# Attention results put in row order by 0/1 matmuls and stored as one transfer of 512-byte rows

## The chip, the cores and the metric

The kernel runs on one core of a Trainium2 chip. The metric is the device time of one execution in microseconds (us). Times are given as the median of several runs. A percentage is the mean time of one kernel's fast runs over that of the other kernel's fast runs of the same rounds, with a 95% interval, so it is not quite the ratio of the medians quoted beside it. In the experiments that mean leaves out each kernel's first, profiled run, which the medians include.

## The reference

Grouped-query attention with 16 batches, 32 query heads on 8 K/V heads, 16 query rows, 2048 keys, D = 128, all bf16:

```python
k = jnp.repeat(k, rep, axis=1); v = jnp.repeat(v, rep, axis=1)   # rep = 4
scores = jnp.einsum("bhqd,bhkd->bhqk", q, k) * D ** -0.5
p = softmax(scores, axis=-1)
return jnp.einsum("bhqk,bhkd->bhqd", p, v)
```

K and V are 67 MB each and are read once; the result is 2.1 MB. One K/V head with its 4 x 16 = 64 query rows is a *group*; there are 128 groups.

## The kernel before

Two groups make a *pair* (64 pairs), two pairs a *step* (32 steps, 4 groups). A static list schedule, computed when the kernel is built, gives each engine a fixed order of operations. SyncE (SP) issues all loads and nearly all stores, in one fixed order; K and V share 15 slots of 1 MB, and a load is issued when its slot comes free.

```python
NSLOT = 15; NBO = 9      # load slots; result buffers O
LAG = 6; DSTORE = 12     # V(p) is loaded 6 pairs after K(p); a store is queued 12 pairs after its V
QCH = 1024; QLEAD = 5    # Q comes in 8 chunks, loaded 5 pairs ahead
# ... the order of SP's transfers:
for t in range(NP + LAG):
    if t < NP:
        dma.append(("K", t))
    if qstep.get(t, 0):
        dma.append(("Q", qstep[t]))
    if t >= LAG:
        dma += v_of(t - LAG)
    if t - LAG - DSTORE in range(0, NP, 2):
        dma.append(("ST", (t - LAG - DSTORE) // 2))
```

For each pair: DVE transposes K in 32x32 blocks, PE makes the scores S, ACT takes the exponential (P), PE transposes P, DVE or ACT evicts that to PT, PE multiplies with V (PV, in `O_ps`), and ACT or DVE scales by 1/rowsum into O. Partition 64·gg + m of an O buffer holds row m of group 4·step + 2·gg + pair, and the two pairs of a step lie side by side in the free dimension:

```python
Osb = [sb(f"O{i}", [128, 2, 128], BF16) for i in range(NBO)]
# ... the normal store of a step (transfers, SP): two transfers, 64 partitions x 2 rows of 256 B each
for gg in range(2):
    g = 4 * x + 2 * gg
    sp.dma_start(of[64 * g:64 * (g + 2), :].rearrange("(p m) d -> m p d", p=2),
                 Osb[x % NBO][64 * gg:64 * (gg + 1), :, :]).then_inc(*prog_sem(prog, op))
# ... at the end, each engine: redo everything in a safe form if a row sum was out of range
eng.br_eq(reg, all_within, on_true=after, on_false=redo).branch_hint(hints[me])
```

Partition m holds row m of two *different* groups, so neither of its two rows has its neighbour in memory beside it: the store is made of 256-byte pieces.

## Time and profile before

| | before |
|---|---|
| time, median | 348.36 us (348.19 to 348.55, 3 runs) |
| span of the profiled execution | 346.9 us |
| DMA | 139.2 MB, 401 GB/s over the span |
| PE, DVE, ACT busy | 69%, 65%, 65% |

The page of the kernel before: the lines of the DMA slices (40 slices of the span; the digit is the busy share in tenths), the packets, the queues (packets, MB, share of 16 engines), and the chain that ended last.

```profile
PE 238.6 (69%) x5378; PEld 172.7 (50%) x5378; DVE 225.8 (65%) x377; ACT 226.6 (65%) x369; POOL 29.0 (8%) x35
...
DMA  7999999999999999999999999999999999999983
GB/s 309 426 412 415 411 413 412 412 415 414 411 418 415 412 412 414 415 413 414 413 412 417 414 415 414 414 413 415 413 413 414 412 417 416 414 412 412 392 336 108
DMA packets 37349, 139.21 MB, mean 401 GB/s; under 512 B 11440, under 2 KB 11440, under 8 KB 29104
...
q1 hardware_dynamic: 37216, 138.41, 98.9%
q8 instruction: 43, 0.70, 0.8%
...
DMA 72%; DVE 11%; PE 9%; ACT 6%; issue 1%; SPq 0%; ACTq 0%
```

DMA is at 9 from the second slice to the 38th, and the chain spends 72% of the span on it, nearly all on loads of K. No compute engine is above 70%. `q8 instruction` is the fetching of instructions in 43 pieces of 16 KB, on the same DMA engines as the loads. The list of issues on the same page (issue, count, size, median time from issue to landing):

```profile
slot<-in_k_dram SPq DMA_DIRECT2D x64, 1024.0 KB, 17.6
...
out_dram<-O SPq DMA_DIRECT2D x62, 32.0 KB, 13.2
```

A megabyte takes 2.5 us to move and lands 17.6 us after its issue: about seven loads are queued at any time. SP's waits for slots therefore cost nothing as long as that queue doesn't run dry.

Busy time by stretch before (windows view: window, length, busy us of each engine with instruction counts, granted clock, DMA share, GB/s):

```profile
110.00:300.00 190.00, 131.95 (x3008) 95.29 (x3008) 121.57 (x204) 127.09 (x210) 15.98 (x16) 0.94 1.03 414
...
324.00:347.00 23.00, 16.75 (x418) 12.96 (x414) 10.30 (x29) 10.57 (x18) 0.00 (x0) 0.95 0.72 260
```

The last K lands at 323.5 us; the last 23 us are a tail in which the last eight pairs get their PV and their result.

### The profile page before, as it was taken

Reading aid. Unit: us, or ns where it says so; the run is one execution under the profiler, and the core shown is the slowest. Engines: PE = TensorE matmul, PEld = TensorE weight load, DVE = VectorE, ACT = ScalarE, POOL = GpSimd, SP = SyncE. Lnnn points to the kernel's source line nnn. Section 1 sums busy time; section 2 is a strip of 40 time slices with the busy share of each in tenths; the row PEclk is TensorE's granted clock in tenths of the full one; section 3 lists DMA queues with packets and bytes.
Section 4 is the critical chain, followed back from the end, with each engine's and each line's share of the span. In section 5 each row is a group of like instructions: output and inputs, shape, how many; then the busy total and the mean of one; then the engine's idle time right before and its main releaser. Section 6 shows DMA issues by size and latency. Waiting matters only on the chain.

```text
span 346.9 us, 11937 instructions
## 1 busy us (share of the span) xinstructions
PE 238.6 (69%) x5378; PEld 172.7 (50%) x5378; DVE 225.8 (65%) x377; ACT 226.6 (65%) x369; POOL 29.0 (8%) x35
## 2 busy tenths in 40 slices
PE   1568868756686668766687665865857757576785
PEld 1345646534464446543465453643645545454564
DVE  4867996874775666746666655767559476576544
ACT  4496887665586575946759646787558746477551
POOL 1310031000400004000040000400004000000000
PEclk9998999999899898999989989999899989899899
DMA  7999999999999999999999999999999999999983
GB/s 309 426 412 415 411 413 412 412 415 414 411 418 415 412 412 414 415 413 414 413 412 417 414 415 414 414 413 415 413 413 414 412 417 416 414 412 412 392 336 108
DMA packets 37349, 139.21 MB, mean 401 GB/s; under 512 B 11440, under 2 KB 11440, under 8 KB 29104
## 3 DMA queue, kind: packets, MB, share of 16 engines
q1 hardware_dynamic: 37216, 138.41, 98.9%
q8 instruction: 43, 0.70, 0.8%
q14 instruction: 10, 0.08, 0.1%
q10 hardware_dynamic: 80, 0.02, 0.0%
HBM read 136.31 MB, written 2.10 MB: 399 GB/s over the span
## 4 chain that ended last, share of the span: by engine, by line
DMA 72%; DVE 11%; PE 9%; ACT 6%; issue 1%; SPq 0%; ACTq 0%
DMA slot<-in_k_dram 72%; DVE KT L354 9%; PE O_ps L468 3%; ACT P L373 2%; PE PT_ps L462 2%; PE S_ps L452 2%; PE QT_ps L440 1%; ACT QT L399 1%; DVE PT L399 1%; ACT PT L399 1%; DMA Qn<-in_q_dram 1%; DVE O L390 1%; ACT L360 0%; ACT Qr L360 0%; DVE rowsum L379 0%
## 5 line engine op out<-in xcount | busy, mean ns | idle before, releaser
L354 DVE STREAM_TRANSPOSE KT<-slot 128x1024 int32<-128x1024 int32 x128 | 154.5, 1231 | 101.3 <-DMA slot<-in_k_dram 92.8
L373 ACT ACTIVATE P<-S_ps 128x1024 bf16<-128x1024 f32 x128 | 130.5, 1025 | 87.5 <-PE PT_ps L462 49.6
L462 PE MATMUL PT_ps<-ident,P 128*128 128x128 bf16 x1024 | 74.4, 229 | 83.1 <-DVE PT L399 44.0
L462 PEld LDWEIGHTS PT_ps<-ident,P 128*128 128x128 bf16 x1024 | 62.3, 102 | 104.7 <-DVE PT L399 53.7
L452 PE MATMUL S_ps<-KT,QT 32*64 32x512 bf16 x2048 | 75.9, 401 | 11.0 <-ACT P L373 9.7
L468 PE MATMUL O_ps<-slot,PT 128*64 128x128 bf16 x2048 | 76.7, 233 | 1.3 <-DVE O L390 1.0
L468 PEld LDWEIGHTS O_ps<-slot,PT 128*64 128x64 bf16 x2048 | 65.9, 119 | 17.8 <-issue 14.2
L399 ACT ACTIVATE PT<-PT_ps 128x1024 bf16<-128x1024 bf16 x60 | 61.1, 1019 | 3.0 <-PE PT_ps L462 2.1
L360 POOL COPY Qr<-Qn 128x1024 bf16<-128x1024 bf16 x28 | 28.0, 1042 | 235.2 <-DMA Qn<-in_q_dram 235.2
L399 DVE COPY PT<-PT_ps 128x1024 bf16<-128x1024 bf16 x68 | 45.2, 668 | 1.8 <-PE PT_ps L462 1.8
L452 PEld LDWEIGHTS S_ps<-KT,QT 32*64 32x64 bf16 x2048 | 28.1, 106 | 32.3 <-ACT P L373 12.9
L440 PE MATMUL QT_ps<-ident,Qr 128*128 128x128 bf16 x256 | 22.1, 236 | 10.2 <-ACT Qr L360 6.1
L399 ACT ACTIVATE QT<-QT_ps 128x1024 bf16<-128x1024 bf16 x23 | 23.5, 1023 | 7.3 <-PE QT_ps L440 7.3
L373 ACT ACTIVATION_READ_ACCUMULATOR P<-S_ps 128x1 f32 x128 | 25.9, 202 | 0.0
L440 PEld LDWEIGHTS QT_ps<-ident,Qr 128*128 128x128 bf16 x256 | 16.7, 105 | 16.5 <-issue 8.3
L388 ACT ACTIVATE O<-O_ps,rrec 128x128 bf16<-128x128 f32 x27 | 9.9, 367 | 11.6 <-PE O_ps L468 11.6
L390 DVE TENSOR_SCALAR O<-O_ps,rrec 128x128 bf16<-128x128 f32 x37 | 12.0, 324 | 5.5 <-PE O_ps L468 5.4
L399 DVE COPY QT<-QT_ps 128x1024 bf16<-128x1024 bf16 x9 | 10.9, 1209 | 1.8 <-PE QT_ps L440 1.8
L379 DVE TENSOR_TENSOR rowsum<-rhalf 128x1 f32<-128x1 f32 x64 | 8.5, 152 | 4.4 <-ACT P L373 4.4
L384 DVE RECIPROCAL rrec<-rowsum 128x1 f32<-128x1 f32 x64 | 8.5, 153 | 0.5
L360 ACT ACT_TABLE_LOAD x1 | 1.3, 1283 | 3.6 <-DMA Qn<-in_q_dram 3.6
L360 DVE COPY Qr<-Qn 128x1024 bf16<-128x1024 bf16 x2 | 1.3, 690 | 3.5 <-DMA Qn<-in_q_dram 3.5
(13 smaller groups left out, 4.2 us busy)
## 6 DMA issues: line engine op xcount, KB each, us to landing
slot<-in_k_dram SPq DMA_DIRECT2D x64, 1024.0 KB, 17.6
slot<-in_v_dram SPq DMA_DIRECT2D x63, 1024.0 KB, 17.7
Qn<-in_q_dram SPq DMA_DIRECT2D x8, 256.0 KB, 15.3
out_dram<-O SPq DMA_DIRECT2D x62, 32.0 KB, 13.2
slot<-in_v_dram SPq DMA_DIRECT2D x2, 512.0 KB, 12.3
out_dram<-O SPq DMA_DIRECT2D x3, 16.0 KB, 1.8
out_dram<-O ACTq DMA_DIRECT2D x1, 16.0 KB, 2.0
```

Of the source, the lines that this page charges most:

```text
L354: ins = eng.transpose(KT[p % NKT][:, gg, :, h], prog.slot(("K", 2 * p + gg))[:, J * 64 * h:J * 64 * (h + 1)])
L360: ins = eng.activation(dst, src, ACT.Copy) if me == "act" else eng.tensor_copy(dst, src)
L373: ins = eng.activation(P[p % 2][:, :].rearrange("m (r a h j) -> m h a r j", h=2, a=2, j=32)[:, h], src.rearrange("m (a r j) -> m a r j", a ...
L379: ins = eng.tensor_tensor(rowsum[:, p:p + 1], rhalf[:, p, 0:1], rhalf[:, p, 1:2], op=ALU.add)
L384: ins = eng.reciprocal(rrec[:, p:p + 1], rowsum[:, p:p + 1])
L388: ins = eng.activation(dst, src, ACT.Copy, scale=r)
L390: ins = eng.tensor_scalar(dst, src, r, None, op0=ALU.mult)
L399: ins = eng.activation(dst, src, ACT.Copy) if me == "act" else eng.tensor_copy(dst, src)
L440: ins = pe.transpose(QT_ps[:, 128 * i:128 * (i + 1)], Qr[:, x, i, :], ident[:, :],)
L452: ins = pe.matmul(S_ps[64 * gg:64 * (gg + 1), 512 * a:512 * (a + 1)], QT[c % 2][32 * a:32 * (a + 1), x, row:row + 64], kt[:, :, x // 2, p ...
L462: ins = pe.transpose(PT_ps[h][:, 128 * t:128 * (t + 1)], P[p % 2][:, 128 * r:128 * (r + 1)], ident[:, :])
L468: ins = pe.matmul(O_ps[64 * gg:64 * (gg + 1), 0:128], PT[p % NPT][:, r, 64 * gg:64 * (gg + 1)], prog.v_rows(p)[:, gg, r, :], start=(r == 0 ...
```

## The change

The intent: make the store cheaper for the DMA engines. For each step, 8 small matmuls with columns of the identity (weights 0 and 1) copy O into PSUM so that each partition holds two neighbouring rows; an eviction writes them to `Orow`; one transfer of 128 partitions x 512 B, contiguous in memory, stores the step. The matmuls borrow the PSUM bank `QT_ps` of the Q transposes, so Q chunks must fit between two steps, and Q is loaded 10 pairs ahead instead of 5. Cut to its core:

```diff
+NOS = 3
-NBO = 9
+NBO = 7
-DSTORE = 12
+DSTORE = 10
-QLEAD = 5
+QLEAD = 10
...
+            add(("op", s), ("nm", p - 1), ("nm", p), opt(s >= 1, ("oe", s - 1)), ("qe", chunk, 3))
+            add(("oe", s), ("op", s), opt(s >= NBO, ("ST", s - NBO)))
+            add(("ST", s), ("oe", s))
...
+    O_rows = QT_ps[:, 0:512].bitcast(F32)
...
-                for gg in range(2):
-                    g = 4 * x + 2 * gg
-                    sp.dma_start(of[64 * g:64 * (g + 2), :].rearrange("(p m) d -> m p d", p=2),
-                                 Osb[x % NBO][64 * gg:64 * (gg + 1), :, :]).then_inc(*prog_sem(prog, op))
-                continue
+                dst = of[256 * x:256 * (x + 1), :].rearrange("(a e) d -> a (e d)", e=2)
+                src = Orow[x % NBO][:, :, :].rearrange("a e d -> a (e d)")
...
+            elif kind == "op":
+                for e in range(2):
+                    for gg in range(2):
+                        for pp in range(2):
+                            x = 64 * gg + 32 * pp
+                            ins = pe.matmul(
+                                O_rows[x:x + 32, 128 * e:128 * (e + 1)], ident[:, 64 * gg + e:64 * gg + 64:2],
+                                Osb[p % NOS][:, pp, :], start=True, stop=True, tile_position=(0, x), ...
```

(Cut: the dependencies that order the Q transposes against `op`, the semaphore counts, one scratch tensor moved into another.) The last step is stored as before.

## The prediction

> **What bounds the kernel now.** DMA. The page's slices show the DMA digit at 9 from slice 2 to 38, at 411 to 418 GB/s; the chain of waits puts 72% of the span on loads of K. PE is at 69%, DVE and ACT at 65%. By the list of DMA issues 6 to 9 loads are in flight when the next is issued, 15 to 20 us before it lands, so the queue's waits for free slots cost nothing. The last K lands at 323.5 us; the timeline then shows a 23 us tail in which PE, ACT and DVE wait for each other, while the last V halves land at 342.0 and 343.3, just as PE needs them.
>
> **What the stores cost.** The packet records give 18 ns for each of 8192 packets of 256 B, 84 ns for 2 KB, 309 ns for 8 KB: 9 ns fixed and 9.4 ns per 256 B. The Trainium skill (DMA: Bandwidth & Descriptors, "Why small descriptors are slow") has a fixed overhead per packet for 256-byte descriptors; the trace agrees (0.070 ns/B against 0.038 at 8 KB). Two stores of one step take 16 packets and 2 semaphore writes (9 ns) on each DMA engine: 306 ns. After: 8 packets of 512 B (28 ns, an estimate by that fit) and one semaphore write: 233 ns. Over 31 steps that is at most 2.3 us. But stores cost less than their packet times: reads ran at 412 GB/s in 20 to 60 us (no stores) and 408 in 110 to 300 us, and the first engine's landings are 2.50 to 2.54 us apart without and 2.64 with a store between: near 0.13 us per step, 3.3 us before the last K. The change saves a quarter to a half of that: 0.8 to 1.6 us.
>
> **What is added.** 31 times 8 matmuls: PV's 32 take 1.08 us, so about 0.3 us each time, 9 us of PE; and 31 evictions of 128x256 f32: from 128 and 1024 columns on ACT (367 and 1019 ns) an estimate of 0.46 us, 14 us over ACT and DVE, idle a third of the time. In the steady part none is on the critical path. In the tail two or three groups compete with the last pairs: +0.3 to 1 us. 496 more PE instructions are some two more 16 KB instruction fetches (43 now), each of which sets one DMA engine back by about 1.5 us (landings of one load spread over 0.4 us before the first fetch, 8 us at the end): 0 to 0.5 us.
>
> **New waits.** The row-order matmuls share QT_ps with the Q transposes: a chunk's four transposes and evictions (9 us in series) must fit between two of them, some 10 us apart. Stores after a chunk may be a few us late, and loads behind them in the queue. With 12 us of queue DMA should not run dry.
>
> **Prediction.** 348.4 - 1.2 (stores) + 0.4 (tail, fetches) + 0 (steady compute) = 347.6 us; 345.8 to 349.4. Faster by over 2%: 0.03; same: 0.94; slower: 0.03.
>
> **Right or wrong, by step.** 7,936 packets of 256 B become 3,968 of 512 B at about 28 ns; reads in 110 to 300 us rise from 408 toward 410 GB/s; the last K lands about 1 us earlier; PE busy +9 us, DVE plus ACT +14; the tail is 0 to 1 us longer.
>
> **What would make it wrong.** A DMA slice below 9 between 40 and 320 us: the queue ran dry behind a late store (up to +5 us). Stores that cost reads more than their packets show, so that mending them gives 3 us or more. A new static order that moves the tail by over 2 us.

## The result, and the profile after

Over six runs of each, the kernel after took 348.71 us (348.25 to 349.17) against 348.40 us (347.86 to 348.98) before: ratio 1.0009, interval 0.9996 to 1.0022. The change moved nothing that these runs can tell from zero.

The page after, the same lines as above:

```profile
PE 250.4 (72%) x5626; PEld 177.1 (51%) x5626; DVE 238.7 (69%) x402; ACT 224.0 (65%) x375; POOL 29.6 (9%) x35
...
DMA  8999999999999999999999999999999999999983
GB/s 313 424 417 411 412 411 413 410 418 411 413 419 415 414 415 415 416 412 413 417 411 414 415 416 417 414 413 419 410 412 420 414 414 416 412 418 413 409 323 108
DMA packets 32887, 139.24 MB, mean 402 GB/s; under 512 B 3008, under 2 KB 6976, under 8 KB 24640
...
q1 hardware_dynamic: 32752, 138.41, 98.4%
q8 instruction: 45, 0.74, 0.9%
...
DMA 56%; PE 20%; ACT 10%; DVE 8%; issue 2%; SPq 2%; ACTq 0%
```

The change did what it set out to do: packets under 512 B fell from 11440 to 3008 (7936 pieces of results and 496 semaphore writes), and 3968 packets of 512 B took their place. The rate did not answer: 402 GB/s instead of 401, the same digits in every slice but the first. The chain's share of DMA fell from 72% to 56%, but that is only another path through the same waits: the DMA slices show that DMA was as busy as before. The groups and issues that are new (group: busy us, mean ns of one; then the idle time before it):

```profile
L476 PE MATMUL QT_ps<-O,ident 128*32 128x128 bf16 x248 | 9.2, 226 | 19.8 <-DVE O L404 17.2
...
L415 DVE CAST Orow<-QT_ps 128x256 bf16<-128x256 f32 x24 | 9.7, 406 | 1.4 <-PE QT_ps L476 1.4
...
slot<-in_k_dram SPq DMA_DIRECT2D x64, 1024.0 KB, 19.7
...
out_dram<-Orow SPq DMA_DIRECT2D x31, 64.0 KB, 17.9
```

The windows after:

```profile
110.00:300.00 190.00, 138.45 (x3184) 98.56 (x3168) 129.77 (x217) 127.86 (x217) 13.90 (x14) 0.94 1.02 415
...
324.00:347.00 23.00, 16.67 (x412) 12.01 (x410) 10.97 (x32) 9.05 (x16) 0.00 (x0) 0.95 0.67 254
```

The added work sits where it was expected (PE +6.5 us and DVE +8.2 us in 110 to 300 us), the tail's busy times are about as before (ACT 1.5 us less), and the DMA queue stayed deep (K lands 19.7 us after its issue). So neither a dry queue nor a longer tail shows. The following times are worked out from the trace's records: a load is moved by 16 DMA engines, each of which reports its own completion, so a load has a first and a last landing.

| one profiled execution each | last K, first / last engine (us) | last V half, first / last (us) | span (us) |
|---|---|---|---|
| before | 315.36 / 323.55 | 335.56 / 343.33 | 346.9 |
| after | 315.00 / 323.05 | 334.54 / 342.73 | 346.4 |

The last K came 0.5 us earlier. The profiled execution of the kernel after was, at 348.25 us, the fastest of its six, and that of the kernel before (348.72) one of the slower; such tables are good for mechanisms, not for tenths of a microsecond.

Note the spread between first and last engine: 8 us in both kernels. Until 20 us all 16 engines land a load within 0.5 us. Then jumps of about 1.5 us appear, on one engine at a time, mostly soon after a 16 KB instruction fetch starts (the first at 23.0 us). The Trainium skill (Runtime: NRT & Kernel Launch, "Instruction fetch mechanics") says that instructions are fetched in blocks of 16 KiB and that crossing into the next costs one DMA tail-bump, "mostly hidden". The 43 fetches agree with the block size. The loads are not spared: when the last K of the kernel before had landed, 39 fetches had started, and the eight late landings of that load were together 60 us behind its first one, 1.5 us for each fetch. The first eight landings lay within 2.7 us. So the fetches seem to fall on eight of the 16 DMA engines, and that would be why eight run late; the landing records do not name their engine, so this is inferred.

### The profile page after: what moved, and what is told of

It reads as the page before. It is cut to its first block, busy times and chain, and to the rows that moved or that the text cites. A ratio compares the mean times of both kernels' runs of the same rounds, so it can differ in the third digit from the quotient of the medians.

```text
span 346.4 us, 12427 instructions
## 1 busy us (share of the span) xinstructions
PE 250.4 (72%) x5626; PEld 177.1 (51%) x5626; DVE 238.7 (69%) x402; ACT 224.0 (65%) x375; POOL 29.6 (9%) x35
## 2 busy tenths in 40 slices
DMA packets 32887, 139.24 MB, mean 402 GB/s; under 512 B 3008, under 2 KB 6976, under 8 KB 24640
## 4 chain that ended last, share of the span: by engine, by line
DMA 56%; PE 20%; ACT 10%; DVE 8%; issue 2%; SPq 2%; ACTq 0%
DMA slot<-in_k_dram 49%; ACT P L387 6%; PE S_ps L465 6%; DMA slot<-in_v_dram 6%; PE PT_ps L485 6%; PE O_ps L491 6%; DVE KT L368 5%; SPq L442 2%; PE QT_ps L453 2%; ACT QT L415 2%; DVE PT L415 1%; ACT PT L415 1%; DVE QT L415 1%; DMA Qn<-in_q_dram 1%; DVE O L404 1%
## 5 line engine op out<-in xcount | busy, mean ns | idle before, releaser
L465 PE MATMUL S_ps<-KT,QT 32*64 32x512 bf16 x2048 | 78.9, 416 | 10.4 <-ACT P L387 9.2
L415 ACT ACTIVATE PT<-PT_ps 128x1024 bf16<-128x1024 bf16 x54 | 55.0, 1019 | 3.3 <-PE O_ps L491 1.9
L415 DVE COPY PT<-PT_ps 128x1024 bf16<-128x1024 bf16 x74 | 48.7, 669 | 2.3 <-PE PT_ps L485 1.8
L465 PEld LDWEIGHTS S_ps<-KT,QT 32*64 32x64 bf16 x2048 | 28.6, 109 | 33.6 <-ACT P L387 11.8
L415 ACT ACTIVATE QT<-QT_ps 128x1024 bf16<-128x1024 bf16 x21 | 21.4, 1021 | 8.2 <-PE QT_ps L453 8.2
L402 ACT ACTIVATE O<-O_ps,rrec 128x128 bf16<-128x128 f32 x34 | 12.5, 369 | 18.4 <-PE O_ps L491 18.3
L476 PE MATMUL QT_ps<-O,ident 128*32 128x128 bf16 x248 | 9.2, 226 | 19.8 <-DVE O L404 17.2
L476 PEld LDWEIGHTS QT_ps<-O,ident 128*32 128x32 bf16 x248 | 3.8, 95 | 27.6 <-DVE O L404 20.2
L404 DVE TENSOR_SCALAR O<-O_ps,rrec 128x128 bf16<-128x128 f32 x30 | 9.8, 325 | 7.1 <-PE O_ps L491 6.8
L415 DVE COPY QT<-QT_ps 128x1024 bf16<-128x1024 bf16 x11 | 13.2, 1204 | 1.4 <-PE QT_ps L453 1.4
L415 DVE CAST Orow<-QT_ps 128x256 bf16<-128x256 f32 x24 | 9.7, 406 | 1.4 <-PE QT_ps L476 1.4
## 6 DMA issues: line engine op xcount, KB each, us to landing
slot<-in_k_dram SPq DMA_DIRECT2D x64, 1024.0 KB, 19.7
Qn<-in_q_dram SPq DMA_DIRECT2D x8, 256.0 KB, 17.6
out_dram<-Orow SPq DMA_DIRECT2D x31, 64.0 KB, 17.9
```

What stands on the lines that cost most here:

```text
L402: ins = eng.activation(dst, src, ACT.Copy, scale=r)
L404: ins = eng.tensor_scalar(dst, src, r, None, op0=ALU.mult)
L415: ins = eng.activation(dst, src, ACT.Copy) if me == "act" else eng.tensor_copy(dst, src)
L465: ins = pe.matmul(S_ps[64 * gg:64 * (gg + 1), 512 * a:512 * (a + 1)], QT[c % 2][32 * a:32 * (a + 1), x, row:row + 64], kt[:, :, x // 2, p ...
L476: ins = pe.matmul(O_rows[x:x + 32, 128 * e:128 * (e + 1)], ident[:, 64 * gg + e:64 * gg + 64:2], Osb[p % NOS][:, pp, :], start=True, stop= ...
```

## The experiments

Theory 1: a store costs the DMA engines about 0.13 us a step whatever its packets, and the eight DMA engines that run late at the end pace the kernel, so it matters *which* engines a store uses. I believed that the two stores of a step ran on different halves of the engines. Theory 2 came out of the first four runs: part of a store's packet time is paid, the store shape gains about 0.5 us, and the added work loses it again. Rivals are stated with each run. Twelve kernels ran, with 5 rounds each.

### No steady stores at all

```diff
+            if kind == "ST" and x < NP // 2 - 1:
+                continue
```

(and no operation waits for these stores; the result is wrong)

> The kernel before without its 31 steady pairs of stores (62 transfers of 32 KB; wrong result on purpose): the most that any better store could give. Theory 1 (a store costs the DMA engines about 0.13 us for each pair, whatever its packets, some 25 pairs before the last K): last K lands about 3.3 us earlier, time about 345.3 us against 348.4. Rival (stores are hidden by the reads of HBM and cost nothing): within 0.5 us of before.

Measured: 345.16 us against 348.34, ratio 0.9904 (0.9891 to 0.9918), so 3.3 us. The last K landed at 312.15 (first engine) and 321.13 (last), 3.2 and 2.4 us earlier than before (the traced run, 346.45 us, was the slowest of its five). From the trace's records, reads (2 to 8 KB packets of SP's queue, 110 to 300 us) ran at 411.0 GB/s against 405.7 before.

What follows: the stores do cost, 0.107 us a step, and it reaches the end of the kernel. **3.3 us, 1.0%, is all that any better store could give in this schedule** (SP's issues and waits for the stores go with them, so it is an upper bound). By packet durations, two stores take 306 ns of each DMA engine in a step, 9.5 us in all; only a third of that is paid. The DMA queues' shares add up to a little more than 16 engines' span (101.7% for SP's queue in 110 to 300 us), so packets overlap, and packet time is not engine time.

### Both stores of a step from the low half, or from the high half, of the partitions

```diff
-                                 Osb[x % NBO][64 * gg:64 * (gg + 1), :, :]).then_inc(*prog_sem(prog, op))
+                                 Osb[x % NBO][0:64, :, :]).then_inc(*prog_sem(prog, op))
```

(the other run has `[64:128, :, :]`; wrong results)

> Before, with both stores of each pair read from partitions 0 to 63 (wrong result on purpose; same packets, bytes and issues). Theory 1 (partitions 0 to 63 are served by the eight DMA engines that run 5 to 8 us ahead at the end, and the eight behind set the time): the late engines lose all store work, last K about 3 us earlier, 345.5 us. Rival (all 16 engines share each store, or the time does not hang on the late engines): 348.4 within 0.5 us.

> The mirror: both stores of each pair read from partitions 64 to 127 (wrong result on purpose). Theory 1: the late engines get twice the store work, last K about 3 us later, 351.5 us, and the landings of one load spread over 13 us or more at the end instead of 8. Rival: 348.4 within 0.5 us.

Measured: 348.11 us (0.9994, 0.9981 to 1.0008) and 348.49 us (1.0007, 0.9993 to 1.0020). Nothing moved, and the landings of the last K are those of before within 0.3 us.

What follows: the part of theory 1 on partitions is wrong; each store uses all the engines alike. The two stores of a step count on the *same* semaphore. The profile gives the first 16 of its 32 increments to the first store and the rest to the second. As eight engines ran 3 to 8 us ahead, the first 16 increments were the early engines' shares of *both* stores, and I read two sets of engines where there was one.

### The store part alone

```diff
-                for gg in range(2):
-                    g = 4 * x + 2 * gg
-                    sp.dma_start(of[64 * g:64 * (g + 2), :].rearrange("(p m) d -> m p d", p=2),
-                                 Osb[x % NBO][64 * gg:64 * (gg + 1), :, :]).then_inc(*prog_sem(prog, op))
-                continue
+                dst = of[256 * x:256 * (x + 1), :].rearrange("(a e) d -> a (e d)", e=2)
+                src = Osb[x % NBO][:, :, :].rearrange("a e d -> a (e d)")
```

(before's schedule, nothing added; the rows come out in the wrong order)

> The store part of the change alone: before's schedule, each pair of stores replaced by one transfer of 128 rows of 512 B read straight from O (rows in the wrong order on purpose), no matmuls and no evictions added. Theory 1 (the cost of a store goes by its bytes; packet size and shape save next to nothing): 348.2, 0.0 to 0.4 us below before. Rival A (the store shape does save the 1.2 us predicted and the added work gives it back): 347.2.

Measured: 347.83 us against 348.34, ratio 0.9985 (0.9972 to 0.9999), 0.5 us with an interval of 0.0 to 1.0. It lies between the two expectations (0.0 to 0.4, and 1.2), much nearer to theory 1's; rival A's 1.2 lies outside the interval. The packets do what the prediction said: 512 B took 27 ns each, against 18 ns for 256 B. A step then takes 8 x 27 + 9 = 225 ns of each engine instead of 306, 2.5 us less in 31 steps; a fifth of that is paid out.

What follows: the store shape by itself is worth about 0.5 us, a sixth of the 3.3 us that stores cost, and hardly told from zero.

### The added work alone

From the kernel after: the matmuls, evictions, and early Q loads stay, the stores are before's and don't wait for them.

```diff
-NOS = 3
-NBO = 7
+NOS = 9
+NBO = 9
+NBR = 1
-            add(("oe", s), ("op", s), opt(s >= NBO, ("ST", s - NBO)))
-            add(("ST", s), ("oe", s))
+            add(("oe", s), ("op", s))
+            add(("ST", s), ("nm", p - 1), ("nm", p))
```

(cut: DSTORE back to 12, a wait of the scaling for the store of its buffer, semaphore counts, before's two transfers from `Osb`)

> The other half of the change alone, with a correct result: the 31 groups of 8 row-order matmuls and their evictions are made, the chunk order and the early Q loads of the change are kept, but the stores stay before's (two transfers of 256-byte rows read from O). Theory 2 (the store shape gave the 0.5 us of the run with the store alone, and the added work gives it back): 349.1, 0.4 to 1.2 us above before. Rival (the added work is free; the missing gain is chance in the static order of the after kernel): 348.4 within 0.3 us.

Measured: correct, 349.27 us against 348.61, ratio 1.0028 (1.0011 to 1.0045), 1.0 us by the ratio. What follows: the added work is not free. The two halves add up: -0.15% and +0.28% make +0.13%, where the whole change measured +0.09% (-0.04 to +0.22); each term is uncertain by 0.13 to 0.17%. By these numbers the 0.5 us that the store gives goes into the added work. Where in the kernel that is paid, this trace can't tell: its run (348.85 us) was the fastest of its six.

### Where the added work costs: the last five steps, or the others

```diff
+FROM, TO = 0, 26       # the other run: 26, 31
-            add(("op", s), ("nm", p - 1), ("nm", p), opt(s >= 1, ("oe", s - 1)), ("qe", chunk, 3))
-            add(("oe", s), ("op", s))
+            if FROM <= s < TO:
+                add(("op", s), ("nm", p - 1), ("nm", p), opt(s >= FROM + 1, ("oe", s - 1)), ("qe", chunk, 3))
+                add(("oe", s), ("op", s))
```

(against the kernel of the added work alone; cut: the same bounds in two other dependencies and in PE's last wait)

> The added work alone (as in the run with the work only, which cost 1.0 us), but with the row-order groups of the last 5 steps left out, so that none runs after the last K has landed. Correct result. If the cost is in the tail, where PE, ACT and DVE wait for each other: 348.6 or less, within 0.3 us of before. If it is in the stream (the two further instruction fetches, or the Q loads put ahead of K): 349.3, 0.7 or more above before.

> The complement: only the last 5 steps make their row-order groups and evictions, with before's stores. Correct result. If the cost of the added work is in the tail: 349.3, 0.7 or more above before. If it is in the stream: 348.6, within 0.3 us.

Measured: only the last five steps, 348.59 us against 348.37, ratio 1.0003 (0.9990 to 1.0015). All but the last five, 351.84 us, ratio 1.0098 (1.0084 to 1.0113): far more than the whole of the added work had cost. The trace shows why. The last engine work ended at 344.7 us and the last store landed at 346.65, much as before, but the span lasted until 350.1. The line of the final branch in that kernel (each engine's branch, count, duration min/median/max in ns, start):

```profile
L514 PEldq COMPARE_BRANCH  x1: 4427/4427/4427, 345.3 to 345.3; - x1
```

and the same branch in the kernel before:

```profile
L485 PEldq COMPARE_BRANCH  x1: 482/482/482, 345.1 to 345.1; - x1
```

PE's branch over the code that isn't needed took 4.4 us instead of 0.5. The program hints this branch a fixed number of operations before the end, and here the hint seems to have come to nothing. The skill page named above, same section, says that a taken branch to a target outside the window forces a fetch of the target's page before execution goes on. The trace agrees: in this kernel a 16 KB fetch starts at 346.70 us, in the middle of PE's branch (345.3 to 349.7), and takes 1.6 us; in the kernels before and after no fetch starts during it. Why the hint failed isn't shown.

What follows: the added work costs nothing measurable in the last five steps (at most 0.5 us by the interval), so the tail isn't shown to pay. That run settles one thing more. It keeps the early Q loads (the third to fifth chunk issued at 6.8, 46.7 and 91.3 us, before: 30.7, 73.8 and 118.0) and has a new static order, and it is as fast as before: the early Q loads alone cost nothing measurable. What it lacks are the groups of the first 26 steps and the two further fetches (pages of the whole added work, and of its last five steps alone):

```profile
q8 instruction: 45, 0.74, 0.9%
...
q8 instruction: 43, 0.70, 0.8%
```

That these two pay, or one of them, is left over, but the run that should have shown it is spoilt by an accident of its own. Taking some 3 us off for the branch (the other engines waited for PE from 346.8 us on) would leave about 0.3 us, which is an argument and not a measurement.

### Rows of 128 bytes

Each store is cut into two of half rows (correct results), first for all steps, then for steps 0 to 20 alone.

```diff
+                    for e in range(2):
+                        sp.dma_start(of[64 * g:64 * (g + 2), 64 * e:64 * (e + 1)].rearrange("(p m) d -> m p d", p=2),
+                                     Osb[x % NBO][64 * gg:64 * (gg + 1), :, 64 * e:64 * (e + 1)]
+                                     ).then_inc(*prog_sem(prog, op))
```

> Before with every store cut into two of 128-byte half rows (correct result): same bytes, twice the packets, twice the semaphore writes, 62 more issues. Theory 2 (about a quarter of a store's packet time is paid, 9 ns of each packet being fixed): packet time per engine and pair goes from 306 to about 470 ns, 31 pairs add 5 us of packet time, so 1.2 us more: 349.6. Rival B (only the bytes of a store are paid): 348.4 within 0.3 us. Rival C (rows under 512 B cost a great deal at the HBM): 350 or more.

Measured: 358.26 us, ratio 1.0280 (1.0264 to 1.0296), nearly 10 us more. It looks like rival C, but the last V half landed at 344.96, only 1.6 us later than before. The rest is SP's: its queue in that kernel from 340 us on (start, length, what, how many):

```profile
338.82 13.58 SPq L427 DMA_DIRECT2D out_dram<-O  x18
352.44 1.88 SPq L421 DMA_DIRECT2D out_dram<-O  x3
```

Eighteen issues in 13.6 us, then three more: issuing a transfer of 64 partitions x 2 pieces takes SP 0.6 us and more, and twice as many of them were left to issue when the loads were done. So the run was mended:

> The run with 128-byte half rows repeated with only steps 0 to 20 cut in two; later stores as before, so that the queue that issues them (0.61 us each, which held back the end of that run: last V landed 1.6 us later, the end came 9 us later) has no more to issue at the end. Correct result. Theory 2 (about a quarter of the added packet time is paid): 1.2 to 1.6 us above before, 349.9. If 128-byte rows cost much more at the HBM than that: over 351.

Measured: 349.97 us against 348.37, ratio 1.0051 (1.0035 to 1.0068), so 1.6 us by the medians and 1.8 by the ratio: the expected number, but not the expected share. In 21 steps the packets take 146 ns more of each engine (32 x 13 + 4 x 9 = 452 ns against 306), 3.1 us in all; about half was paid. A quarter, as theory 2 has it, would be 0.8 us, and the expectation's 1.2 to 1.6 doesn't follow from it. SP's 42 further issues are a rival that no run parts from the packets: the median K landed 14.6 us after its issue instead of 17.6. But DMA stayed at 9 from the second slice to the 39th, so no dry queue shows, and the reads in 110 to 300 us ran at 401.8 GB/s against 405.7. What follows: smaller pieces do cost, in the way packet times suggest and at a discount; there is no cliff below 512 B in these runs. From 128 to 256 B the whole of 31 steps would save about 2.4 us (1.6 x 31/21, an estimate), from 256 to 512 B 0.5 us: the number of packets, and with it the fixed part, is halved with each doubling, so most of the gain had been made before this change. The packet times alone (146 and 81 ns a step) would have the second doubling give half as much as the first, not a fifth; the intervals are wide, and the difference stays open.

### A store on eight DMA engines

```diff
-                    sp.dma_start(of[64 * g:64 * (g + 2), :].rearrange("(p m) d -> m p d", p=2),
-                                 Osb[x % NBO][64 * gg:64 * (gg + 1), :, :]).then_inc(*prog_sem(prog, op))
+                    sp.dma_start(of[64 * g:64 * (g + 2), :].rearrange("(m c e) d -> c m (e d)", c=8, e=2),
+                                 Osb[x % NBO][64 * gg:64 * (gg + 1), :, :].rearrange("m p d -> m (p d)"),
+                                 ).then_inc(*prog_sem(prog, op))
```

The Trainium skill (DMA: Bandwidth & Descriptors, "Why a DMA increments its semaphore by 16 and not by 1") says that a transfer is split over the largest number of engines, at most 16, that divides the slowest dimension of both sides. A slowest dimension of 8 rows in memory should give 8.

> Before with each store addressed as 8 blocks of rows (512-byte rows in the wrong order on purpose), which should put it on 8 DMA engines only. At the end 8 engines run up to 8 us ahead of the other 8. If it lands on the early 8: the late ones lose all store work, about as good as no stores, 345.3 us. If on the late 8: about 3 us longer, 351. If on all 16 alike: 347.9 as with the store alone (0.5 below before).

Measured: 351.45 us against 348.61, ratio 1.0084 (1.0068 to 1.0100), the second of the three outcomes in time. That 8 engines were used shows in the count of 4-byte semaphore packets: 2753 instead of 3249, which is 62 x 8 fewer. The 16 landings of the last K, in order (us; from the trace's records):

```
before   first 315.36 ... 8th 318.08, 9th 321.41 ... last 323.55
g_eight  first 316.35 ... 8th 319.02, 9th 319.08 ... 14th 321.79, 15th 326.85, last 326.96
```

The same bytes, on half of the engines: by rank, the 9th to 14th landing came 1.5 to 3.7 us earlier, the last two over 3 us later than the latest had been, and the kernel lost 2.9 us. (The last V half came 2.5 us later, so the loads account for most of that. PE's final branch took 2.3 us here too, but the last store landed after it, at 350.2.) The eight are therefore not simply the late eight, as one of my expectations had it, but seem to include some of the latest. What follows: the end goes with the *last* engine to land, not with the average, which moved by only 0.3 us.

### Stores moved behind the loads

If a step's stores cost 0.107 us while the loads run, they should be free after the last load. One load slot is given up for 16 more O buffers.

```diff
+EXTRA = 1
+NBF = NBO + 16 * EXTRA
+DSTORE_FAST = 34
+BATCHES = [(13, 17), (17, 21), (21, 25), (25, 30), (30, 31)]   # steps stored together after the loads, 4 transfers each
```

> Before (no row-order matmuls, 256-byte rows), correct result: one of the 15 load slots is given up to hold 16 more O buffers, stores are issued 22 pairs later, and 18 of the 31 steps are stored after the last load in batches of 4 transfers for 4 or 5 steps. Theory 2 (a pair of stores in the stream costs 0.107 us, 3.3 us / 31; the queue has slack for one slot; DMA has room after the last V): about 11 pairs fewer before the last K and 13 before the last V half: 347.1, 1.0 to 1.5 us below before. If the slot was needed: equal or slower.

Measured: correct, 356.30 us, ratio 1.0218 (1.0203 to 1.0233). The loads did what was expected (last K 321.76, last V half 341.23, 1.8 and 2.1 us earlier) with one slot fewer. But the last engine work ended at 342.4 and the span at 355.0: again SP, issuing (result transfers in that kernel: issue duration ns min/median/max, first and last start):

```profile
L455 SPq DMA_DIRECT2D out_dram<-O x8: 596/619/1427, 344.6 to 350.0; - x8
L447 SPq DMA_DIRECT2D out_dram<-O x3: 594/595/597, 350.7 to 351.9; - x3
```

A second form gave part of the late stores to GpSimd, with its own queue (8 transfers once V 57 has landed), and left the others to SP singly:

```diff
+BATCHES = [(14, 18), (18, 22)]        # issued by GpSimd
+GATE = 57
```

> The late stores mended: SyncE could not issue 18 steps of 256-byte rows after the last load (the end waited for it). Now 14 steps in the stream, 8 steps stored in 2 batches by GpSimd once V 57 has landed, 9 steps by SyncE at the end as before; still one load slot fewer. Correct result. If stores in the stream cost 0.107 us each step before the last K and room is left in the tail: 1 us below before, 347.4. If the transfers issued by GpSimd crowd out the last V: equal to before or above.

Measured: correct, 353.81 us, ratio 1.0145 (1.0128 to 1.0162). GpSimd's transfers landed by 335.3, and the last V half came no earlier than before (343.11): it kept 0.2 us of the 1.5 us by which the last K was early. SP was still issuing the last 21 transfers until 349.5, and the span ended at 351.9. That is the expectation's second case; whether GpSimd's transfers or SP's after them took the gain back, no run parts. What follows: moving stores out of the loads' way shows in the landings of the last K both times and in that of the last V only the first time; SP's issuing then made both kernels slower than before. In the kernel after, a late store of 64 KB in 512-byte rows took SP a third of a microsecond (its result transfers between 335 and 343 us, same columns):

```profile
L442 SPq DMA_DIRECT2D out_dram<-Orow x2: 332/332/332, 336.4 to 340.6; - x2
```

Late stores of that kind were not tried.

No kernel with a correct result was faster than the kernel before.

## Why the prediction was right or wrong

The measured time, 348.71 us, lies in the predicted range of 345.8 to 349.4, and "within 2%" was right. The sum behind it was 348.4 - 1.2 + 0.4 = 347.6, a gain of 0.8 us; what the runs showed is 348.4 - 0.5 + 1.0, a loss of 0.5 us by the two halves and of 0.3 us, not told from zero, by the whole.

- **"DMA" bounds the kernel; "the queue's waits cost nothing": right.** Taking away 2 MB of stores out of 139 MB moved the end by 3.3 us.
- **"0.13 us per step, 3.3 us before the last K": right in the total.** Measured 3.3 us at the end of the kernel by taking the stores away, 0.107 us for each of 31 steps; the last K came 2.4 to 3.2 us earlier. Reading the loads' rate with and without stores gave a better price for a store than the packets' durations would have (9.5 us).
- **"The change saves a quarter to a half of that: 0.8 to 1.6 us": too much.** This term was mis-sized. The store part alone gave 0.5 us (0.0 to 1.0). The packets were as predicted (3968 of 512 B at 27 ns, predicted 28), but only a fifth of the packet time saved came back as time. Reads in 110 to 300 us rose by 0.3 GB/s (405.7 to 406.0; the prediction's 408 counts the instruction fetches in), not by 2, and the last K came 0.5 us earlier, not 1 us.
- **"+0.4 us (tail, fetches)": too little, and in the wrong place.** The added work alone cost 1.0 us (0.4 to 1.6). Its sizes were right: `op` 9.2 us of PE (predicted 9), evictions 12.4 us (24 x 406 and 7 x 384 ns; predicted 14), two more instruction fetches (43 to 45); PE as a whole was busy 11.8 us more, DVE and ACT together 10.3. But "in the tail two or three groups compete with the last pairs: +0.3 to 1 us" failed: with the work in the last five steps alone the kernel was 0.03% slower than before (-0.10 to +0.15), at most 0.5 us.
- **"In the steady part none is on the critical path": left open.** The run with the last five steps alone keeps the early Q loads and costs nothing measurable, which takes them off the list (at most 0.5 us). The cost must come from the groups of the earlier steps, their further fetches, or the static order that these bring. The run that should have shown it was spoilt by the final branch. In the traces with the added work in the earlier steps the last engine's landing of V 60 is 1 us late and that of the last V half isn't, which fits fetches that come at other moments, but no run isolates it.
- **Queue, new waits: right.** DMA stays at 9 in every slice from the second to the 38th, and a store lands 17.9 us after its issue, a load of K 19.7.

Both errors go the same way: the gain was 0.7 us too high, the cost 0.6 us too low, and the measured time lies 1.1 us above the predicted 347.6. The range was wide enough to hold that (it reached 1.8 us above 347.6), so it was the range that was right, and the small gain it was built around did not come.

## What to carry to other kernels

Before making a transfer cheaper, run the kernel without it: one run with a wrong result gives the most that can be had, here 1.0%, and the best shape gave a sixth of that. Packet durations overlap and overstate what small packets cost; the landings of the loads on either side of a store are the better price. Count what is added outside the engines too: every issue of a transfer (0.6 us of SP) and some 250 further instructions (here 496 on PE brought two more 16 KB fetches, each on a DMA engine that is already full) can lengthen the path that ends last, and an experiment that changes the number of instructions or of issues must first be looked at in its last 10 us.

## What the Trainium skill lacked or had wrong

- DMA: Bandwidth & Descriptors, "Specifications", gives at least 512 B as the smallest transfer for line rate. Here rows of 256 B instead of 512 B cost 0.15% of the kernel (1.5% of its bytes are stores), and 128-byte rows no more than their packets suggest (1.6 us for 21 steps). In the trace a store packet takes 13, 18 and 27 ns for 128, 256 and 512 B; by these durations 512 B moves at 19 B/ns, where 8 KB reads (309 ns) move at 26.5.
- The same page, "Why small descriptors are slow", puts the overhead at 3 cycles in 11 for 256 B. The packet durations here fit a fixed 9 ns in 18 for 256 B; and the page doesn't say that such durations overlap: of 9.5 us of packet time per engine, 3.3 us were paid when mixed with loads.
- The same page, "Issuing engines are not separate DMA queues", calls the time to issue a DMA usually small. With stores of 64 partitions x 2 pieces of 256 B, SP took 0.6 us each (0.33 us for one of 128 pieces of 512 B in the kernel after), and in three experiments this set the end by 5 to 10 us. That section gives no figure, and none by the shape of a transfer.
- Runtime: NRT & Kernel Launch, "Instruction fetch mechanics", calls the fetch mostly hidden. With DMA saturated, the 39 fetches up to the last K fit a delay of 1.5 us each on one engine's loads, and the landings of one load spread from 0.4 to 8 us. The page gives no duration for a branch that has to fetch its target: 4.4 us on PE here, with one fetch of 1.6 us in it, against 0.5.
- No page speaks of what a shared semaphore does to a profile: the landing times of two transfers that count on it can't be told apart.
- No page says which DMA engines fetch instructions. Here 39 fetches fit a delay on eight of the 16 (eight late landings of one load, together 60 us behind).
